# A fourth new order of the same 1382 steps in a one-core delta-rule and gated feed-forward kernel

## The chip, the cores and the metric

The kernel runs on one core of a Trainium2 chip. The metric is the time of one execution in microseconds (us) on the device; the time of a kernel is the median of its runs. The core has five engines that work at once, each taking its own instructions strictly in its own order: PE (TensorE, matrix products into the accumulation memory PSUM), DVE (VectorE), ACT (ScalarE), POOL (GpSimd), and SP (SyncE), which here only starts DMA transfers. An instruction waits until what it reads has been written and what it overwrites has been read, and everything behind it on the same engine waits with it.

## What is computed

A delta-rule attention layer (4 batches, 8 heads, 768 positions, 48 features a head) gives a matrix x of 3072 tokens by 384, and that goes through a gated feed-forward layer:

```python
k_n = k / (np.linalg.norm(k, axis=-1, keepdims=True) + 1e-06)
for t in range(S):
    y[:, :, t] = np.einsum('bhd,bhde->bhe', q[:, :, t], state)
    v_old = np.einsum('bhde,bhd->bhe', state, kt)
    state = state + bt[:, :, :, None] * np.einsum('bhd,bhe->bhde', kt, vt - v_old)
x = attn_out.transpose(0, 2, 1, 3).reshape(B * S, H * D)
a = x @ w1
b = x @ w2
h = a * b @ w3
return (h @ w_out).astype(np.float32)
```

Here kt, vt and bt are the normalised key, the value and the beta of position t. The weights w1 and w2 are 384 by 1024, w3 is 1024 by 1024, w_out 1024 by 384.

## The kernel before

The 768 positions are cut into 12 chunks of 64. Two chunks, of all batches and heads, make a pair; there are six pairs, called 0 to 5, and each gives 512 tokens of x for the feed-forward part. The work is written as generators, each cut by `yield` into steps; a step issues anything from one instruction to some tens on one engine. A string called ORDER lists 1382 steps by name, and the kernel is built by taking the next step of each name in the list. After the list has run, `in_text_order` ties every engine's instructions to the order in which they were written. So the list, and nothing else, sets what each engine does in which order; no scheduler moves anything afterwards. In this text g1.9 is the ninth step of the generator g1.

The generators that the prediction speaks of, with their lines:

- k, q, v, p: loads of keys, queries and values by SP. q1 is the load of the queries of chunk 1 into the tile X (L1233); the kernel needs it for Q1, their transposes on PE (L409).
- P0 to P35: pieces of the weights. Each is one load on SP (L838), two passes on ACT (L846, L849), one on DVE (L851) and one on POOL (L853). t transposes pieces of w3 on PE (L904), with a copy of the result on ACT (L907), and f folds w3 and w_out into one matrix on PE (L913).
- g squares the keys on POOL (L301) and sums the squares on DVE (L303); g.9 brings the sums of a pair together on PE (L286). N makes the norms from them, 15 short operations on DVE in a chain (L310 to L334), and the scale `wt` that the scores need.
- s makes the scores of a chunk: products on PE (L451, L457) into one of two large PSUM tiles ps_w, and from these on DVE U (L463) and PT (L474). u stores U to device memory (Ud, L491), V loads it again in another layout (Ub, L510) and then inverts the blocks in 31 pairs of DVE operations (L524, L529), shortest operands first and last; its result goes back through device memory to e, the corner products on PE (L619).
- n, c and y are the chain of states along the chunks on PE (L672) and DVE (L706, L717, L738), and its outputs (PE L777). y ends with four copies on ACT (L795) and six transfers that bring the feature rows of xT to their places (SP, L806).
- a and b are the products x@w1 and x@w2 (PE L934). Eight steps pairs of a, a20 to a27 for pair 2, make a round: a20.1 is the w1 product, a20.2 its copy by ACT (L946), a20.3 the w2 product, a20.4 the multiplication of the two on DVE (L950). Every product takes the next of four one-bank PSUM tiles ps_f, so a product waits until what the fourth product before it left there has been taken away.
- S are sums of slabs of a*b on POOL (L1007), o the products with the folded matrix on PE (L1166, seven to a pair), x the sums that make the results (DVE L1197, ACT L1201) and their stores on SP (L1182).
- The last pair does the products in another way (PE L1074, ACT L1088 to L1110, DVE L1083 to L1131).

The stages follow each other with overlap: loads and weights up to about 65 us, the products of pair 0 (a0, b) up to 146, the seven o of pair 0 and the states between up to 183, then for each pair a round of 16 products and a stretch of o, s, c and y, and from 496 us on the last pair.

Of the kernel before, what the change touches and what calls it, by code (L numbers as in the profile page):

```python
# [1358 lines left out]
```

## Time and profile before

| | us |
|---|---|
| three runs | 556.41, 562.43, 560.41 |
| their median | 560.41 |
| the profiled execution, first to last instruction | 556.1 |
| DVE busy in it | 343.7 (62%) |
| ACT busy in it | 145.7 (26%) |
| POOL busy in it | 169.7 (31%) |

The profiled execution is a separate one; its span stands 0.3 us under the fastest of the three runs and 4.3 us, 0.8%, under their median. The two lines that follow are of the page's part 2, the span in 40 slices of 13.9 us, each digit the busy share of a slice in tenths:

```profile
PE   6699999999999999999999999999999999989997
DVE  6799738589546498574995354885373973213552
```

PE is below nine tenths in the first two slices, once near the end and in the last slice. DVE is full in some slices, but in most it has room.

### The profile page before, as it was taken

Reading aid. Unit: us, or ns where it says so; the run is one execution under the profiler, and the core shown is the slowest. Engines: PE = TensorE matmul, PEld = TensorE weight load, DVE = VectorE, ACT = ScalarE, POOL = GpSimd, SP = SyncE. Lnnn points to the kernel's source line nnn. Section 1 sums busy time; section 2 is a strip of 40 time slices with the busy share of each in tenths; the row PEclk is TensorE's granted clock in tenths of the full one; section 3 lists DMA queues with packets and bytes.
Section 4 is the critical chain, followed back from the end, with each engine's and each line's share of the span. In section 5 each row is a group of like instructions: output and inputs, shape, how many; then the busy total and the mean of one; then the engine's idle time right before and its main releaser. Section 6 shows DMA issues by size and latency. Waiting matters only on the chain.

```text
span 556.1 us, 19932 instructions
## 1 busy us (share of the span) xinstructions
PE 533.6 (96%) x8732; PEld 390.8 (70%) x8732; DVE 343.7 (62%) x800; ACT 145.7 (26%) x291; POOL 169.7 (31%) x213
## 2 busy tenths in 40 slices
PE   6699999999999999999999999999999999989997
PEld 5556667788998544888444897445995447988897
DVE  6799738589546498574995354885373973213552
ACT  2786567531121120220111211202201102212200
POOL 7574443527730002812102522004540027420000
PEclk9999999999999999999999999999999999999999
DMA  9999956594423593453745453605307222020001
GB/s 189 339 307 230 158 140 150 128 160 55 96 48 55 119 147 72 67 88 89 122 74 100 70 91 80 126 38 83 51 15 154 26 60 38 18 58 1 0 2 57
DMA packets 191527, 54.22 MB, mean 98 GB/s; under 512 B 178928, under 2 KB 185072, under 8 KB 191440
## 3 DMA queue, kind: packets, MB, share of 16 engines
q1 hardware_dynamic: 189328, 52.56, 46.3%
q8 instruction: 68, 1.11, 0.9%
q10 hardware_dynamic: 2112, 0.39, 0.5%
q14 instruction: 19, 0.16, 0.1%
HBM read 41.78 MB, written 9.96 MB: 93 GB/s over the span
## 4 chain that ended last, share of the span: by engine, by line
PE 93%; DVE 3%; issue 2%; DMA 2%; ACT 0%; SPq 0%; DVEq 0%
PE ps_f L934 38%; PE ps_f L1166 20%; PE ps_f L913 7%; PE ps_w L672 6%; PE ps_w L777 4%; PE ps_f L1074 4%; PE ps_w L619 3%; PE ps_w L1074 2%; PE ps_w L451 2%; PE ps_f L369 1%; PE ps_w L457 1%; PE ps_f L904 1%; DMA beta_fm<-in_beta_dram 1%; PE ps_w L409 1%; PE ps_w L1166 1%
## 5 line engine op out<-in xcount | busy, mean ns | idle before, releaser
L934 PE MATMUL ps_f<-xT,w2s 128*128 128x512 f32 (+1 forms) x288 | 106.9, 524 | 0.0
L934 PE MATMUL ps_f<-xT,w1s 128*128 128x512 f32 (+1 forms) x288 | 106.7, 524 | 0.0
L934 PEld LDWEIGHTS ps_f<-xT,w2s 128*128 128x128 f32 x288 | 54.1, 190 | 46.5 <-issue 41.6
L934 PEld LDWEIGHTS ps_f<-xT,w1s 128*128 128x128 f32 x288 | 54.0, 190 | 45.3 <-issue 41.6
L1007 POOL TENSOR_TENSOR ab<-ab 128x256 f32<-128x256 f32 x80 | 56.4, 731 | 78.7 <-DVE ab L950 73.8
L946 ACT COPY ab<-ps_f 128x512 f32<-128x512 f32 (+1 forms) x48 | 24.3, 515 | 134.4 <-PE ps_f L934 130.3
L1166 PE MATMUL ps_f<-w,ab 128*128 128x192 f32 x320 | 57.3, 332 | 1.9 <-DVE osb L1197 1.3
L1166 PEld LDWEIGHTS ps_f<-w,ab 128*128 128x128 f32 x320 | 51.6, 190 | 3.3 <-issue 2.4
L524 DVE TENSOR_TENSOR tb<-Vb,Ub 128x31 f32<-128x31 f32 (+15 forms) x124 | 43.0, 347 | 15.4 <-DMA Ub<-Ud 11.5
L529 DVE TENSOR_TENSOR Vb<-Vb,tb 128x31 f32<-128x31 f32 (+15 forms) x124 | 43.0, 346 | 4.3
L913 PE MATMUL ps_f<-wo,w3T 128*128 128x384 f32 x128 | 43.5, 491 | 0.4 <-ACT w3T L907 0.4
L1166 PE MATMUL ps_f<-room,ab 128*128 128x192 f32 x240 | 42.8, 332 | 0.0
L950 DVE TENSOR_TENSOR ab<-ab,ps_f 128x512 f32<-128x512 f32 (+1 forms) x48 | 27.4, 589 | 24.0 <-PE ps_f L934 24.0
L1166 PEld LDWEIGHTS ps_f<-room,ab 128*128 128x128 f32 x240 | 38.7, 190 | 0.7
L913 PEld LDWEIGHTS ps_f<-wo,w3T 128*128 128x128 f32 x128 | 23.5, 190 | 15.4 <-ACT w3T L907 0.5
L301 POOL TENSOR_TENSOR sq<-ktok 128x384 f32<-128x384 f32 x24 | 19.7, 835 | 43.5 <-DMA out_dram<-osb 16.9
L658 POOL TENSOR_TENSOR vtok<-vtok,n 128x384 f32<-128x384 f32 x24 | 19.8, 832 | 39.5 <-DMA vtok<-in_v_dram 39.5
L635 ACT COPY T<-ps_w 32x512 f32<-32x512 f32 x24 | 13.8, 577 | 67.2 <-PE ps_w L619 46.2
L795 ACT COPY xT<-ps_w 112x256 f32<-112x256 f32 x48 | 14.3, 384 | 65.0 <-PE ps_w L777 61.7
L451 PE MATMUL ps_w<-KQ 48*64 48x128 f32 x320 | 21.9, 274 | 1.8 <-DVE PT L474 1.5
L717 DVE TENSOR_TENSOR X<-ps_w,wt 128x768 f32<-128x768 f32 x12 | 11.5, 956 | 19.4 <-PE ps_w L672 12.9
L1197 DVE TENSOR_TENSOR room<-room,ps_f 128x384 f32<-128x384 f32 (+1 forms) x13 | 7.0, 537 | 26.4 <-PE ps_f L1166 26.4
(170 smaller groups left out, 805.9 us busy)
## 6 DMA issues: line engine op xcount, KB each, us to landing
vtok<-in_v_dram SPq DMA_DIRECT2D x24, 192.0 KB, 4.4
out_dram<-osb SPq DMA_DIRECT2D x23, 192.0 KB, 2.6
ktok<-in_k_dram SPq DMA_DIRECT2D x44, 96.0 KB, 3.4
raw<-in_moe_w_dram SPq DMA_DIRECT2D x8, 512.0 KB, 6.2
raw<-in_moe_w_dram SPq DMA_DIRECT2D x18, 192.0 KB, 4.5
raw<-in_moe_w_out_dram SPq DMA_DIRECT2D x7, 384.0 KB, 5.3
Ud<-U SPq DMA_DIRECT2D x40, 64.0 KB, 2.8
Ub<-Ud SPq DMA_DIRECT2D x5, 512.0 KB, 4.2
```

Of the source, the lines that this page charges most:

```text
L451: pe.matmul(ps[half(z), 0, n : n + 128], lhsT=x[:, 0, :], rhs=x.rearrange("p j t -> p (j t)"), start=True, stop=True,)
L524: dve.tensor_tensor(out=tv, in0=V[:, 0 : s + 1, s : s + 1].to_broadcast([P, s + 1, n]), in1=U[:, s, s + 1 : BS].unsqueeze(1).to_broadcast( ...
L529: dve.tensor_tensor(out=o, in0=o, in1=tv, op=ALU.subtract)
L672: pe.matmul(out(ps, r, h, z), lhsT=lhs(r, h, z), rhs=rhs(r, h, z), start=True, stop=True,)
L777: i = pe.matmul(region(h, z, r), lhsT=lhs, rhs=rhs, start=part[n] not in part[:n], stop=part[n] not in part[n + 1 :],)
L913: pe.matmul(ps[:, 0:DM], lhsT=w3Ts[jc, kc // 4][:, kc % 4 * P : kc % 4 * P + P], rhs=wo(kc), start=(kc == 0), stop=(kc == KF - 1),)
L934: pe.matmul(ps[:].rearrange("p b c t -> p b (c t)"), lhsT=w[:, m, js], rhs=x[:, m, :, c0:c1].rearrange("p b c t -> p b (c t)"), start=(m = ...
L946: act.copy(out=t, in_=ps)
L950: dve.tensor_tensor(out=t, in0=t, in1=ps, op=ALU.mult)
L1007: (dve if u == last else pool).tensor_tensor(out=o_, in0=x_, in1=y_, op=op)
L1074: pe.matmul(ps[:, j, :], lhsT=w[j], rhs=x, start=first and j == 0, stop=j == 1, skip_group_check=not first,)
L1166: pe.matmul(ps[b][:, b, :], lhsT=ab_of(u, HF * f + i, t0), rhs=ws_[w][:, i], start=first and i == 0 and (b == 0 or n == "F"), stop=i == HF ...
```

## The change

The string ORDER is another arrangement of the same names. Every name stands in it as often as before; no generator, tile, buffer or instruction differs. The table of names is one line longer, so all code behind it carries a line number higher by one after the change (L934 becomes L935). The first lines of the table:

```diff
-k0 g0 g0 g0 K0 V0 g0 k1 P12 K0 K0 beta K1 P0 g0 g0 K1 K1 g0 q1 P12 g0 P12 P12 beta g0 g0 beta N0
+k0 K0 k1 K1 K0 K0 K0 g0 g0 g0 g0 g0 V0 s0 P13 P13 P13 P0 beta K1 P13 g0 g0 g0 g0 K1 P0 P0 P0 g0
...
```

Three places show what that does on the engines. The first is the start on SP. The rows are DMA issues in their order: `X<-in_q_dram` is the load q1, `raw`, `qperm`, `kperm` and `spare` are the buffers into which the pieces of w1, w2 and w3 (`in_moe_w_dram`) and of w_out come. Before:

```order
L233 DMA ktok<-in_k_dram 64x8x48 x4
L838 DMA raw<-in_moe_w_dram 128x1024
L1251 DMA beta_fm<-in_beta_dram 16x12x64 x2
L838 DMA raw<-in_moe_w_out_dram 128x768
L1233 DMA X<-in_q_dram 32x8x96 x4
L838 DMA raw<-in_moe_w_dram 128x1024
L838 DMA qperm<-in_moe_w_dram 128x1024
```

The same place after:

```order
L234 DMA ktok<-in_k_dram 64x8x48 x4
L839 DMA raw<-in_moe_w_dram 128x1024
L839 DMA raw<-in_moe_w_out_dram 128x768
L1252 DMA beta_fm<-in_beta_dram 16x12x64 x2
L839 DMA raw<-in_moe_w_dram 128x1024
L839 DMA raw<-in_moe_w_out_dram 128x768
L839 DMA qperm<-in_moe_w_dram 128x1024
L839 DMA raw<-in_moe_w_dram 128x1024
L839 DMA spare<-in_moe_w_out_dram 128x768
L839 DMA raw<-in_moe_w_out_dram 128x768
L1234 DMA X<-in_q_dram 32x8x96 x4
```

The queries of chunk 1 are loaded behind eight weight pieces, where they stood behind two.

The second place is PE near 87 us, around g1.9 (`ps_f<-ss,ident`, the sums from which N1 makes the scale of pair 1). Before, with the fold f6 (L913), the transposes Q3 (L369) and a state product c1.3 (L672) between it and the second scores step of s2 (L451, L457):

```order
L286 MATMUL ps_f<-ss,ident 64x16 x2
L913 MATMUL ps_f<-wo,w3T 128x384 x8
L369 MATMUL ps_f<-ident,X 48x2x32 x32
L672 MATMUL ps_w<-R,TT_89 64x48 x32
L451 MATMUL ps_w<-KQ 64x128 x2
L457 MATMUL ps_w<-KQ 64x64 x4
```

The same place after, with one product of b4 (L935) between it and the first scores step of s2:

```order
L778 MATMUL ps_w<-KQ,S 48x64 x16
L287 MATMUL ps_f<-ss,ident 64x16 x2
L935 MATMUL ps_f<-xT,w1s 128x256 x3
L452 MATMUL ps_w<-KQ 64x128 x2
L458 MATMUL ps_w<-KQ 64x64 x4
```

The fold, the transposes and the state product stand ahead of the sums now, and the outputs of y1 (L778) too.

The third place is PE before the products of round 2, from 250 us on: o1.5, o1.6 and o1.7 (L1166, with `room` or `w_117` the weights), the state products c5.3, c5.5 and c6.1 (L672) and the outputs y5.1 (L777), whose transfers fill the xT that round 2 (L934) reads. Before:

```order
L672 MATMUL ps_w<-R,TT_89 64x48 x32
L1166 MATMUL ps_f<-room,ab 128x192 x8
L777 MATMUL ps_w<-KQ,S 48x64 x16
L777 MATMUL ps_w<-PT,X 48x64 x32
L777 MATMUL ps_w<-KQ,S 48x64 x16
L1166 MATMUL ps_f<-room,ab 128x192 x8
L672 MATMUL ps_w<-X,ktok 48x48 x32
L1166 MATMUL ps_f<-w_117,ab 128x192 x8
L672 MATMUL ps_w<-S,KQ 64x48 x32
L286 MATMUL ps_f<-wt,ident 64x16 x2
L934 MATMUL ps_f<-xT,w1s 128x512 x9
```

The same place after:

```order
L1167 MATMUL ps_f<-room,ab 128x192 x8
L673 MATMUL ps_w<-R,TT_89 64x48 x32
L1167 MATMUL ps_f<-room,ab 128x192 x8
L778 MATMUL ps_w<-KQ,S 48x64 x16
L778 MATMUL ps_w<-PT,X 48x64 x32
L778 MATMUL ps_w<-KQ,S 48x64 x16
L673 MATMUL ps_w<-X,ktok 48x48 x32
L1167 MATMUL ps_f<-w_117,ab 128x192 x8
L673 MATMUL ps_w<-S,KQ 64x48 x32
L935 MATMUL ps_f<-xT,w1s 128x512 x3
```

Both o with `room` stand ahead of y5.1 now, where one stood behind it, the first of them ahead of c5.3 as well, and the small product with `ident` (N3.2) has moved out.

The rest, in words. In round 2 the first multiplication on DVE, a20.4, stands behind 18 of the 31 pairs of the inversion V3, where the first one, a25.4, stood behind 16; its product a20.3 is the second of the round, where a25.3 was the fourth. In round 3 the first multiplication stands behind all 31 pairs of V4 in both orders. On PE the products of a round come in another sequence in every round; the sequence within the last pair hardly differs.

More of the change, by code (lines that the diff above doesn't have):

```diff
@@ L64 @@
-x1 S1 x1 S1 y4 S1 y4 c5 o1 d7 d7 d7 d7 s7 s7 k8 g4 s7 s7 s6 s7 s7 u7 s6 s6 s6 s6 s6 c5 S1 c5 o1
-u6 y5 S1 x1 V3 o1 S1 x1 x1 c5 S1 y5 y5 S1 x1 V3 k9 S1 g4 c5 x1 x1 p8 V3 V3 V3 V3 V3 o1 c6 x1 V3
-V3 N3 N3 V3 V3 V3 V3 V3 V3 a27 a27 a25 x1 g4 a20 a25 a20 V3 V3 a25 a25 p8 a22 a22 V3 a24 a21 g4
-V3 V3 V3 a24 V3 d8 d8 p9 v6 V3 V3 a21 g4 g4 V3 V3 V3 V3 V3 V3 V3 V3 a22 a22 a27 a27 a20 n6 a20
-V3 e6 g4 a26 a26 a26 a24 d8 a21 n6 c6 e6 a26 d8 e7 a24 e6 e6 p9 g4 g4 g4 s8 N4 s8 a23 a23 s8 e6
-S2 e7 a21 e6 a23 a23 c6 e7 e7 c6 v7 o2 v9 o2 n7 n7 S2 y6 S2 S2 S2 V4 x2 K2 N4 c6 c6 o2 y6 e7 S2
@@ new lines @@
+d5 c3 n3 v5 c3 o0 x0 x0 x0 c3 c3 y3 y3 x0 x0 s4 N2 o0 s4 s4 s4 s4 s4 s5 s5 x0 s5 s5 s5 s5 y3
+a14 a16 a16 a14 a14 a14 c3 c3 a11 a15 a11 a15 u4 u5 V2 V2 v4 n4 n4 n5 n5 V2 a13 V2 V2 V2 V2 V2
+V2 p6 p6 x0 V2 V2 V2 V2 V2 V2 V2 V2 V2 V2 V2 V2 V2 V2 V2 V2 V2 V2 V2 V2 V2 V2 V2 a17 a17 a12
+a10 c4 a12 a13 d6 a10 a10 a10 S1 a12 a12 a17 a11 a11 a15 N2 a17 k6 g3 c4 g3 g3 g3 k7 g3 g3 g3
+a13 V2 e4 e4 e4 a15 a16 d6 d6 d6 g3 N2 g3 e4 e4 e4 a13 o1 c4 e5 e5 e5 e5 a16 V3 p7 S1 S1 S1 S1
+S1 o1 S1 c4 c4 g3 N3 x1 e5 e5 o1 c4 c5 c5 y4 y4 o1 p7 d7 d7 d7 d7 s7 s7 s7 s7 s7 s7 s6 s6 s6 s6
@@ new lines @@
+u7 s6 u6 x1 S1 S1 S1 S1 S1 S1 S1 x1 o1 x1 c5 c5 s6 o1 x1 y5 y5 c5 x1 S1 S1 o1 c5 c6 V3 V3 V3 x1
+x1 y5 V3 V3 V3 x1 x1 x1 k8 k9 V3 V3 V3 V3 V3 V3 V3 V3 g4 V3 V3 V3 V3 V3 a20 a20 a20 a20 a27 a22
+a22 a24 a24 a27 a24 a26 V3 V3 p8 d8 V3 a24 V3 V3 V3 V3 V3 V3 v6 n6 n6 c6 a26 a26 a26 d8 V3 V3
+p8 d8 d8 V3 a23 a23 a23 a23 a21 v8 V3 g4 g4 g4 a21 a21 a22 a27 g4 g4 S2 g4 g4 g4 V3 e6 e6 e6
+a22 a21 e6 a25 a25 a27 e6 e6 p9 p9 e7 v7 s8 N3 N3 g4 N4 s8 s8 o2 x2 c6 c6 a25 n8 a25 S2 S2 y6
+y6 e7 e7 S2 S2 S2 S2 o2 n8 S2 n7 c6 c6 S2 S2 V4 S2 n7 S2 o2 S2 S2 S2 S2 e7 e7 e7 c7 c7 o2 k11
@@ new lines @@
+c7 c7 d9 d9 s8 s8 u8 s8 x2 x2 o2 d9 d9 y7 y7 y7 x2 o2 x2 x2 s9 s9 s9 s9 o2 s9 u9 x2 x2 x2 x2 V4
+x2 a34 a34 a36 a31 a31 V4 V4 a36 a35 a35 V4 V4 V4 V4 V4 a30 a37 a37 V4 V4 a30 V4 V4 V4 V4 V4
+a32 a32 a33 a33 V4 V4 V4 V4 V4 V4 V4 V4 V4 V4 N4 N4 V4 V4 c7 V4 V4 V4 V4 V4 s9 a30 a30 a34 a34
+p10 d10 a35 a33 d10 a31 p10 a35 a36 k10 g5 g5 c7 c8 V4 e8 e8 e8 c8 g5 g5 a31 a33 a37 e8 e8 a37
+a36 a32 d10 d10 e9 e9 e9 a32 e8 c8 c8 e9 o3 x3 e9 e9 S3 S3 g5 g5 c8 c8 o3 S3 c9 o3 v9 g5 n9 g5
+n9 x3 c9 S3 S3 S3 S3 S3 g5 g5 y8 y8 S3 S3 p11 d11 d11 W p11 d11 c9 c9 v11 x3 N5 v10 n10 S3 S3
@@ L88 @@
+x4 x4 x4 S4 o4 a50 a51 X5 X5 x4 x4 X5 a50 a50 a50 a50 a50 a50 a50 a50 a50 a50 X5 a50 a50 a50
+a50 a50 a50 a50 a50 a50 a50 a51 a51 a51 a51 a51 a51 a51 a51 a51 a51 a51 a51 a51 a51 W a51 a51
+a51 a51 a51 a51 a52 a52 a52 a52 a52 a52 a52 a52 a52 a52 a52 a52 a52 a52 a52 a52 a52 a53 a53 a52
+a52 a52 a53 a52 a53 a53 a53 a53 a53 a53 a53 a53 a53 a53 a53 a53 a53 a53 a53 a53 o5 x5 a53 a53
+o5 S5 S5 o5 o5 S5 S5 K1 S5 S5 S5 S5 o5 x5 x5 x5 o5 x5 x5 x5 x5 x5 o5 x5 x5 Q3 K0 K2 x5 x5 K1 Q2
+Q1 Q2 x5
 """
```

65 lines of the change are left out of this document (24 added, 41 removed).

## The prediction, made before the changed kernel had run

> **What bounds the kernel now.** I read the page's engine line first, then the windows of busy time by stage, then PE's waits, and the timelines only where PE stands still. The engine line, with each engine's busy time:
>
> ```profile
> PE 533.6 (96%) x8732; PEld 390.8 (70%) x8732; DVE 343.7 (62%) x800; ACT 145.7 (26%) x291; POOL 169.7 (31%) x213
> ```
>
> A new order removes no work from PE, so all that it can give or take lies in the 556.1 - 533.6 = 22.5 us in which PE is idle. The windows say in which stages (columns: stretch, its length, busy us of PE, PE's weight loads, DVE, ACT and POOL, granted clock, DMA share, GB/s):
>
> ```profile
> 0.00:14.00 14.00, 8.62 (x220) 7.16 (x221) 8.76 (x21) 3.59 (x5) 9.99 (x22) 1.00 0.97 190
> 14.00:28.00 14.00, 8.30 (x324) 7.24 (x323) 10.88 (x30) 10.98 (x22) 7.30 (x7) 1.00 0.91 340
> 28.00:38.00 10.00, 9.48 (x34) 5.79 (x35) 9.62 (x30) 9.33 (x19) 7.28 (x7) 1.00 0.88 288
> 65.00:113.00 48.00, 46.25 (x1268) 35.28 (x1267) 25.29 (x55) 29.79 (x59) 18.70 (x17) 1.00 0.62 138
> 113.00:163.00 50.00, 49.51 (x727) 44.23 (x725) 34.59 (x91) 11.00 (x24) 28.79 (x36) 1.00 0.60 97
> 163.00:215.00 52.00, 50.86 (x712) 31.72 (x703) 36.04 (x95) 8.16 (x18) 0.00 (x0) 1.00 0.53 90
> 215.00:270.00 55.00, 53.27 (x1306) 41.58 (x1305) 37.17 (x88) 8.60 (x19) 19.30 (x27) 1.00 0.47 90
> 270.00:302.00 32.00, 32.00 (x128) 14.15 (x128) 25.49 (x58) 3.52 (x6) 4.91 (x6) 1.00 0.58 95
> 465.00:496.00 31.00, 29.37 (x789) 27.22 (x779) 7.17 (x12) 6.85 (x16) 12.15 (x18) 1.00 0.08 21
> 534.00:556.10 22.10, 18.55 (x114) 18.23 (x112) 9.08 (x16) 0.96 (x2) 0.00 (x0) 1.00 0.11 36
> ```
>
> 11.6 us are lost in the first 38 us, 1.75 from 65 to 113, 0.5, 1.1 and 1.7 in the next three stretches, nothing in round 2 itself, 1.6 before the last pair and 3.5 at the end. The largest losses by name:
>
> ```profile
> PE ps_w L409 <- issue: 5.4, 2, 4.4
> PE ps_f L1166 <- DVE osb L1197: 1.3, 1, 1.3
> PE ps_w L672 <- DVE X L717: 0.5, 1, 0.5
> ```
>
> So the path is PE from 28 us on, and the question is, stage by stage, whether PE still finds its operands and PSUM tiles ready. I count only PE's idle time, before and after.
>
> **A, the start (-1.0).** PE's rows there, then ACT's, then the sizes of the loads and their time to land:
>
> ```profile
> 21.37 1.06 PE L409 MATMUL ps_w<-KQ 48*32 48x64 f32 x52 [4.42 <-issue]
> 22.37 1.96 PE L369 MATMUL ps_f<-ident,X 64*48 64x64 f32 x64
> 28.05 2.85 PE L913 MATMUL ps_f<-wo,w3T 128*128 128x384 f32 x8 [0.43 <-ACT w3T L907]
> 31.36 1.09 PE L904 MATMUL ps_f<-ident,w 128*128 128x128 f32 x8 [0.47 <-POOL w L853]
> 40.56 1.11 PE L369 MATMUL ps_f<-ident,X 64*48 64x64 f32 x64
> ...
> 16.11 0.68 ACT L846 ACTIVATE w<-raw 128x512 f32<-128x512 f32 x1 [4.27 <-DMA raw<-in_moe_w_dram]
> 27.40 0.60 ACT L907 COPY w3T<-ps_f 128x512 f32<-128x512 f32 x1
> ...
> ktok<-in_k_dram SPq DMA_DIRECT2D x44, 96.0 KB, 3.4
> raw<-in_moe_w_dram SPq DMA_DIRECT2D x8, 512.0 KB, 6.2
> raw<-in_moe_w_out_dram SPq DMA_DIRECT2D x7, 384.0 KB, 5.3
> X<-in_q_dram SPq DMA_DIRECT2D x16, 96.0 KB, 4.9
> ```
>
> The fold f0 at 28.05 waits for ACT's copy at 27.40, and behind it PE loses 0.47 more. After the change ACT has about 1.7 us more ahead of that copy. But it waits less at 16.11: one pass pair of 1.1 us falls into the gap of 4.27, and the weight piece waited for has no q1 ahead of it (4 x 96 KB, 2.0 us at 190 GB/s). The copy comes at 26.0 to 28.0, and I take f0 at 28.0. PE has then done the 8.62 + 8.30 us of before and t5 (0.93) besides: idle 28.0 - 17.85 = 10.15, and 0.45 for the next transposed piece, where it was 11.6. The ends are -3.0 (copy at 26.0) and +1.5 (below).
>
> What q1's move costs: behind eight pieces it ends the first 4,736 KB (8 x 96 of keys, 4 x 512 and 4 x 384 of weights, 4 x 96 of its own), 4.85 MB. At 190 GB/s for 14 us, then 340, these are in at 14 + (4.85 - 2.66)/0.34 = 20.4 us. PE takes from Q1 to f0 22.37 to 28.05 less 0.43, and t5: 6.1 us. Q1 must start by 21.9. So q1 lies beside other work, by 1.5 us.
>
> The 4.42 us that end at 21.37 come from no operand that the trace shows. They may move with the order; the time they take lies ahead of the copy at 27.40 and gives nothing alone. The 64 transposes at 22.37 take 1.96 us, the same 64 at 40.56 take 1.11, while the windows give the clock as 1.00 in both. [...]
>
> **B, the second scores (+0.9).** From the sums g1.9 to the first U of s2, DVE's first and last row:
>
> ```profile
> 88.18 0.16 DVE L291 COPY ss<-ss 128x16 f32<-128x16 f32 x1
> 93.05 0.69 DVE L463 TENSOR_TENSOR U<-ps_w,wt 128x512 f32<-128x512 f32 x1
> ```
>
> This chain takes 4.9 us, and with U and PT (0.69 and as much) some 6.5 to 6.9 us from the sums until the first ps_w tile is free for s3. Before, a fold of 5.4 us covered it. Now PE has two half products b4.1 and b7.1 (1.3 each, half of a product below) and the two steps of s2 (0.95 each): 4.5. PE waits 2.0 to 2.4, I take 2.0. With 0.6 for corner products that come just behind their operands, this stage loses 2.6 instead of 1.75. Ends +0.3 and +1.5.
>
> **C, 113 to 183 us (-0.4).** The wait of L672 for DVE's X goes (0.5, the waits above), since o0.4 now stands between; y3.1 directly behind c3.3 brings most of it back, and N2 ahead of s4's multiplications makes s5.1 wait where s5.4 did. 1.3 instead of 1.7. Ends -0.8 and +0.3.
>
> **D, the way to round 2 (0).** PE's waits in this stretch, then what leads to xT (ACT's copies behind y5.1, SP's transfers, their landing), then the chain's row of a whole run of products:
>
> ```profile
> 250.37 1.15 PE L672 MATMUL ps_w<-R,TT 64*64 64x48 f32 x59 [0.20 <-DVE PT L474]
> 251.84 0.32 PE L672 MATMUL ps_w<-R,TT 64*64 64x48 f32 x5 [0.33 <-issue]
> 256.57 0.67 PE L777 MATMUL ps_w<-KQ,S 48*48 48x64 f32 x32
> 261.36 2.84 PE L1166 MATMUL ps_f<-w,ab 128*128 128x192 f32 x16 [0.46 <-DVE tb L524]
> ...
> 257.29 1.20 ACT L795 COPY xT<-ps_w 112x256 f32<-112x256 f32 x4 [13.52 <-PE ps_w L777]
> ...
> 258.51 4.22 SPq L806 DMA_DIRECT2D xT<-xT  x6
> ...
> xT<-xT SPq DMA_DIRECT2D x30, 32.0 KB, 2.0
> ...
> 265.36 36.25 PE ps_f L934 x84
> ```
>
> The three waits, 1.0 in all, go: with o1.5 and o1.6 ahead, operands and tiles are ready. But y5.1 ended at 257.24 and the fourth of its six transfers landed at about 258.51 + 3/6 x 4.22 + 2.0 = 262.6, 5.4 us later, the last 6.9 later. The first product needs the fourth, its end the sixth. Before, o1.6 (2.8) stood behind y5.1 too; now only c5.5, o1.7 and c6.1 do, 0.9 + 2.8 + 1.0 = 4.7. PE waits 0.7 to 2.2, I take 0.9: what was won is lost again. Ends -0.3 and +1.2.
>
> **E, round 2 (+0.2).** The rows of V3 on DVE (the first and the last of the pairs that matter, and one between), and POOL's at the same time:
>
> ```profile
> 263.74 0.25 DVE L524 TENSOR_TENSOR tb<-Vb,Ub 128x87 f32<-128x87 f32 x1
> 274.86 1.09 DVE L524 TENSOR_TENSOR tb<-Vb,Ub 128x256 f32<-128x256 f32 x1
> 278.62 0.42 DVE L529 TENSOR_TENSOR Vb<-Vb,tb 128x252 f32<-128x252 f32 x1
> ...
> 274.84 0.83 POOL L301 TENSOR_TENSOR sq<-ktok 128x384 f32<-128x384 f32 x1 [3.88 <-DVE Vb L529]
> ```
>
> a20.4 stands behind pair 18 of V3, and a24.3, the sixth product, wants the tile that a20.4 empties. V3's third pair comes at 263.2 (behind o1.7's last matmul and one sum). From 263.74 to 279.04 it took 15.3 us, 1.2 of which are other operations that have moved: 14.1, so the pair ends at 277.3 and a20.4 at 277.9. PE starts a20.1 at 265.36 less 0.5 (A to C), 0.2 (the small product that moved out) and the 1.0 of D, plus 0.9: 264.6. It comes to a24.3 five products of 2.59 later (36.25 / 14, six rows each), 277.5. The 1.09 at 274.86 is 0.66 over its neighbours and falls on the square on POOL. [...] I take 0.2, between nothing and 0.4; ends -0.2 and +1.5.
>
> **F and G, rounds 3, 4 and the last pair (+0.2, +0.2).** a31.3 waits for a tile that DVE empties just behind V4; in round 4 all tiles are free some us early; a50.3 has one product less to cover ACT's copy. The 1.3 us of L1166 on DVE's sums and the end's 3.5 keep their order. Each end -0.2 and +1.0.
>
> **The sum.** -1.0 + 0.9 - 0.4 + 0 + 0.2 + 0.2 + 0.2 = +0.1, so the profiled 556.1 become 556.2. The median of the runs stands 4.3 above that execution; 560.41 + 0.1 gives 560.5.
>
> **Rivals.** (1) Slower: q1 lands late. Past 21.9 us every us of q1 is a us of PE. For it: all of the eight pieces stand ahead of it on one queue, and a piece takes 5 to 6 us to land. Against: 340 GB/s were reached in this stretch. It decides from 21.9 on; landing at 28.0 costs 6.1: 566.6. (2) Slower, but less: V3 itself starts late, because its load of Ub stands behind a store of results on SP. Each us beyond a start of 263 is a us at a24.3 and again at the tiles behind it; 3 us give 563.5. Against: nothing in round 2 waits now. (3) Faster: the start runs without the 4.42 stall and the copies come early too: 11.6 idle becomes 6.5, 555.4. Against: ACT's row at 27.40 is full behind 16.11. (4) The change does nothing that can be seen is what I forecast; the moves on DVE, ACT and POOL are hidden behind a PE that is busy 96%.
>
> **Chances.** Forecast 0.62, within 557 and 564; rival 1 0.13; rival 2 0.12; rival 3 0.13. The three runs shown spread over 6 us, so a result can stand 2 to 3 us off by that alone. The range takes rival 3 to its time and rival 1 nearly to its: 555.0 to 566.5. A measurement tells about 1%, 5.6 us, from no change. Below 554.8 lies most of half of rival 3 and a spread: 0.10. Above 566.0 lie rival 1 and a part of rival 2: 0.16. Within: 0.74.
>
> **What would show it.** In the profile after: f0's first product at 28 (A right) or past 30 (rival 1, with PE's wait ahead of L369 named after the DMA into X); a wait of about 2 us of L451 on DVE's PT near 100; the waits at c5.3 and o1.7 gone and one of 0.7 to 2.2 us of the first L934 product on the xT transfers; at the sixth product of round 2 less than 1 us on DVE. PE's idle time altogether 22 to 23 us. I am wrong if it is below 18 or above 27.

## The result and the profile after

The kernel after takes 576.23 us (median of four runs, 575.20 to 577.52), the kernel before in the same session 559.73 (four runs, 556.41 to 562.43). The ratio is 1.0306, with a 95% interval of 1.0258 to 1.0354: slower by 3%, some 17 us. The forecast was 560.5, and 566.5 was the upper end of its range. In two of the experiments below (norms and q1 together; V1's late copy) some executions were slower than the rest (585.45 and 583.64 against 577.87 and 574.41 us; 583.19 against 573.88 to 577.60), so their ratios are of the others, and the trace of the first, taken in the one of 585.45, is used for its first 33 us and where it is named.

The profiled execution of after spans 573.5 us, 17.4 more than that of before. The engine line of its page, each engine with its busy time:

```profile
PE 537.2 (94%) x8732; PEld 391.3 (68%) x8732; DVE 355.3 (62%) x800; ACT 146.0 (25%) x291; POOL 171.2 (30%) x213
```

The same 8732 matmuls take 3.6 us more, and PE is idle for 573.5 - 537.2 = 36.3 us instead of 22.5. The windows of four stages (columns as in the prediction's: stretch, length, busy us of PE, its weight loads, DVE, ACT, POOL, granted clock, DMA share, GB/s) and the largest of PE's waits by name that grew or are new (us in all, times, longest):

```profile
0.00:14.00 14.00, 6.56 (x221) 5.58 (x222) 8.17 (x15) 5.52 (x9) 10.13 (x22) 1.00 0.92 217
14.00:28.00 14.00, 8.83 (x251) 7.62 (x250) 10.36 (x26) 7.09 (x14) 5.98 (x5) 0.51 1.06 339
28.00:38.00 10.00, 8.34 (x97) 5.70 (x98) 9.41 (x26) 9.94 (x21) 6.16 (x6) 1.00 0.88 254
...
113.00:163.00 50.00, 45.02 (x328) 39.11 (x326) 35.28 (x93) 6.99 (x18) 20.99 (x24) 0.97 0.54 86
...
PE ps_w L410 <- issue: 7.2, 2, 4.5
PE ps_f L935 <- DVE ab L951: 5.6, 2, 5.0
PE ps_w L620 <- issue: 1.8, 2, 1.0
PE ps_f L935 <- DMA xT<-xT: 1.7, 2, 0.9
PE ps_f L905 <- ACT KQ L380: 1.6, 1, 1.6
```

The first, in which PE waits for nothing that the trace shows, was there before and has grown from 5.4 to 7.2; the other four are new. The largest rise of idle time is in the last of these stretches, 5.0 us where before had 0.5.

Since the two kernels do their work in different order, windows of time compare unlike things. A better measure is the time that PE has lost up to a given step: the start of the step, less the time that the PE steps ahead of it took in the profiled execution of before. It holds idle time and slowed matmuls alike. The columns are the amounts of PE work that before has done at 40, 56, 70, 123, 145, 183 and 279 us, and the last product; all from the steps' starts in the traces.

| PE's lost time, us, up to | 40 | 56 | 70 | 123 | 145 | 183 | 279 | end |
|---|---|---|---|---|---|---|---|---|
| before | 12.0 | 11.6 | 11.7 | 13.3 | 13.3 | 15.0 | 16.7 | 19.0 |
| after | 15.1 | 15.4 | 16.4 | 20.4 | 27.2 | 29.4 | 33.6 | 36.7 |
| after, V1's second copy early | 15.3 | 15.0 | 16.0 | 20.3 | 20.4 | 22.8 | 27.1 | 31.2 |
| after, norms first | 17.8 | 18.9 | 19.8 | 23.4 | 31.7 | 33.4 | 37.6 | 41.0 |
| after, q1 early | 18.7 | 17.8 | 19.0 | 21.7 | 29.6 | 32.0 | 39.5 | 43.8 |
| before's order to f0.2 | 11.9 | 18.1 | 19.3 | 22.1 | 29.9 | 32.8 | 37.0 | 40.3 |
| the same, copy early, v1 and q2 late | 11.7 | 12.4 | 14.4 | 18.2 | 18.3 | 20.7 | 27.3 | 33.7 |
| before, v1 and q2 early | 11.6 | 13.9 | 13.9 | 15.2 | 15.2 | 16.6 | 17.7 | 20.1 |
| before's order to g1.9, copy early | 12.0 | 11.7 | 11.7 | 16.3 | 16.4 | 18.8 | 23.2 | 27.9 |
| before's order to c1.5, copy late | 12.0 | 11.7 | 11.5 | 19.4 | 27.2 | 29.9 | 34.0 | 37.8 |
| before's order to o0.1 | 11.9 | 11.6 | 12.1 | 14.2 | 14.2 | 17.8 | 21.4 | 25.0 |
| the same, y5.1 ahead of o1.6 | 11.7 | 11.4 | 11.3 | 12.6 | 12.6 | 15.7 | 23.1 | 28.8 |
| the same, all of y5 ahead of o1.6 | 11.6 | 11.3 | 11.0 | 13.2 | 13.2 | 20.5 | 31.9 | 35.3 |

After loses 17.7 us more than before: 3.1 by 40 us, 1.6 more by 70, 2.4 by 123, then 6.8 at once by 145 (27.2 - 20.4, where before lost nothing), and 3.8 behind that. Executions of one order differ too: the last three rows share their order up to o1.6, and stand 5 us apart at 183. In the last of them the granted clock was 0.57 from 176 to 184 us, 1.00 in the other two, and the 16 matmuls of an o there took 4.87 us, 3.03 in the first of the three. So a difference of a few us in this table says nothing without a row of a timeline behind it.

The start in the timeline of after (columns: start, length, instruction, and in brackets the idle time before it and what ended it), first PE, then DVE and POOL:

```profile
16.01 0.85 PE L410 MATMUL ps_w<-KQ 48*32 48x64 f32 x35 [4.50 <-issue]
16.79 0.40 PE L287 MATMUL ps_f<-ss,ident 64*64 64x16 f32 x4
17.12 1.45 PE L1259 MATMUL ps_f<-ident,beta_fm 16*128 16x16 f32 x12
18.50 1.37 PE L410 MATMUL ps_w<-KQ 48*32 48x64 f32 x77
22.61 1.06 PE L410 MATMUL ps_w<-KQ 48*32 48x64 f32 x51 [2.74 <-issue]
29.13 1.21 PE L905 MATMUL ps_f<-ident,w 128*128 128x128 f32 x8 [1.56 <-ACT KQ L380]
...
20.79 1.26 DVE L311 TENSOR_SCALAR seed<-ss 128x32 uint32<-128x32 uint32 x1
22.09 1.23 DVE L318 SCALAR_TENSOR_TENSOR nt<-ss,seed 128x32 f32<-128x32 f32 x1
...
20.74 1.28 POOL L854 TENSOR_TENSOR w<-w,raw 128x512 uint32<-128x512 uint32 x1 [0.42 <-ACT spare L850]
21.98 1.29 POOL L854 TENSOR_TENSOR w<-w,qperm 128x512 uint32<-128x512 uint32 x1
```

The first stall stands now inside s0.1, ahead of the sums of the keys (16.79, at 12.25 before) from which N0 makes the norms; a second one follows in s1. Two of N0's short operations take 1.2 us each, exactly beside POOL's work on weight pieces. N0 is done at 26.4, where it was at 16.6: 4.5 us of that lie ahead of its sums, 3.2 are passes over weight pieces that DVE does ahead of the chain, and 2.1 the two slow operations. The first fold starts at 32.06 instead of 28.05.

The second place is V1, the inversion of the next pair's blocks. SP's load, ACT's two copies of V1, DVE's first pair and the product that waits for it, from the timeline of after:

```profile
116.42 0.34 SPq L511 DMA_DIRECT2D Ub<-Ud  x1
...
120.98 0.60 ACT L519 COPY ps_w<-Vb 128x512 f32<-128x512 f32 x1
127.46 0.60 ACT L519 COPY ps_w<-Vb 128x512 f32<-128x512 f32 x1
...
128.09 0.19 DVE L525 TENSOR_TENSOR tb<-ps_w,Ub 128x31 f32<-128x31 f32 x1 [5.59 <-ACT ps_w L519]
...
147.65 3.24 PE L935 MATMUL ps_f<-xT,w2s 128*128 128x256 f32 x7 [4.97 <-DVE ab L951]
```

DVE has nothing else to do from 122.5 on, but the second of the two copies, step V1.4, stands on ACT behind the copies of four products (b1, b0, a04, b3), and each of these waits for PE. DVE stands still for 5.59 us. The multiplications of the products stand on DVE behind V1's pairs, so 20 us later PE waits 4.97 us for an emptied tile. The seven matmuls behind the wait are slow as well (last section): some 1.6 us more, which with the wait is nearly all of the 6.8.

The third place is the way to round 2:

```profile
275.16 1.20 ACT L796 COPY xT<-ps_w 112x256 f32<-112x256 f32 x4 [15.01 <-PE ps_w L778]
...
276.38 4.16 SPq L807 DMA_DIRECT2D xT<-xT  x6
...
280.81 1.10 PE L935 MATMUL ps_f<-xT,w1s 128*128 128x512 f32 x2 [0.77 <-DMA xT<-xT]
282.83 1.96 PE L935 MATMUL ps_f<-xT,w1s 128*128 128x512 f32 x4 [0.92 <-DMA xT<-xT]
```

The wait for xT that term D foresaw is there, 1.7 us.

### The profile page after: what moved, and what is told of

It is laid out like the page before. It is cut to its first block, busy times and chain, and to the rows that moved or that the text cites. A ratio compares the mean times of both kernels' runs of the same rounds, so it can differ in the third digit from the quotient of the medians.

```text
span 573.5 us, 19927 instructions
## 1 busy us (share of the span) xinstructions
PE 537.2 (94%) x8732; PEld 391.3 (68%) x8732; DVE 355.3 (62%) x800; ACT 146.0 (25%) x291; POOL 171.2 (30%) x213
## 3 DMA queue, kind: packets, MB, share of 16 engines
q8 instruction: 68, 1.11, 0.8%
## 4 chain that ended last, share of the span: by engine, by line
PE 72%; DVE 19%; issue 3%; DMA 3%; SPq 1%; ACT 1%; POOL 0%; DVEq 0%; POOLq 0%; ACTq 0%
PE ps_f L935 29%; PE ps_f L1167 18%; DVE tb L525 5%; PE ps_w L673 5%; PE ps_w L778 4%; PE ps_f L1075 4%; DVE ps_w L530 3%; PE ps_w L1075 2%; PE ps_w L620 2%; DVE Vb L530 2%; PE ps_f L914 2%; PE ps_w L452 1%; DMA raw<-in_moe_w_dram 1%; PE ps_w L458 1%; DVE w L852 1%
## 5 line engine op out<-in xcount | busy, mean ns | idle before, releaser
L935 PE MATMUL ps_f<-xT,w2s 128*128 128x512 f32 (+1 forms) x288 | 109.3, 531 | 5.6 <-DVE ab L951 5.6
L935 PE MATMUL ps_f<-xT,w1s 128*128 128x512 f32 (+1 forms) x288 | 106.7, 524 | 1.7 <-DMA xT<-xT 1.7
L935 PEld LDWEIGHTS ps_f<-xT,w2s 128*128 128x128 f32 x288 | 54.9, 194 | 51.6 <-issue 40.1
L935 PEld LDWEIGHTS ps_f<-xT,w1s 128*128 128x128 f32 x288 | 54.0, 190 | 47.8 <-issue 44.7
L302 POOL TENSOR_TENSOR sq<-ktok 128x384 f32<-128x384 f32 x24 | 20.1, 847 | 111.0 <-DVE tb L525 40.4
L525 DVE TENSOR_TENSOR tb<-Vb,Ub 128x31 f32<-128x31 f32 (+15 forms) x124 | 44.4, 358 | 11.2 <-DMA Ub<-Ud 7.4
L530 DVE TENSOR_TENSOR Vb<-Vb,tb 128x31 f32<-128x31 f32 (+15 forms) x124 | 45.0, 363 | 4.3
L951 DVE TENSOR_TENSOR ab<-ab,ps_f 128x512 f32<-128x512 f32 (+1 forms) x48 | 27.3, 590 | 19.4 <-PE ps_f L935 19.3
L914 PEld LDWEIGHTS ps_f<-wo,w3T 128*128 128x128 f32 x128 | 23.4, 190 | 15.6 <-ACT w3T L908 0.7
L525 DVE TENSOR_TENSOR tb<-ps_w,Ub 128x31 f32<-128x31 f32 (+15 forms) x62 | 21.1, 340 | 7.2 <-ACT ps_w L519 5.6
L739 DVE TENSOR_TENSOR S<-S,ps_w 112x768 f32<-112x768 f32 x10 | 9.5, 952 | 21.8 <-PE ps_w L673 21.6
L530 DVE TENSOR_TENSOR ps_w<-ps_w,tb 128x31 f32<-128x31 f32 (+15 forms) x62 | 21.7, 349 | 2.1
```

The lines of the kernel that those rows point to most:

```text
L302: pool.tensor_tensor(out=sq[:], in0=kt[:, r], in1=kt[:, r], op=ALU.mult)
L525: dve.tensor_tensor(out=tv, in0=V[:, 0 : s + 1, s : s + 1].to_broadcast([P, s + 1, n]), in1=U[:, s, s + 1 : BS].unsqueeze(1).to_broadcast( ...
L530: dve.tensor_tensor(out=o, in0=o, in1=tv, op=ALU.subtract)
L914: pe.matmul(ps[:, 0:DM], lhsT=w3Ts[jc, kc // 4][:, kc % 4 * P : kc % 4 * P + P], rhs=wo(kc), start=(kc == 0), stop=(kc == KF - 1),)
L935: pe.matmul(ps[:].rearrange("p b c t -> p b (c t)"), lhsT=w[:, m, js], rhs=x[:, m, :, c0:c1].rearrange("p b c t -> p b (c t)"), start=(m = ...
L951: dve.tensor_tensor(out=t, in0=t, in1=ps, op=ALU.mult)
```

## The experiments

Each kernel is an arrangement of the same steps, with one exception that is named; V1.4 is the fourth step called V1, and so on. Line numbers differ by one or two from those of after. The ratios are to the kernel before in the same session (557.8 to 558.5 us). A diff shows the names of ORDER around the moved ones, or tells of which parts a mixed order is made.

**V1's second copy.** V1.4 stands directly behind V1.3.

```diff
- V1 V1 P24 b1 b1 a04 b0 b0 a04 b3 b3 V1 a01 a01
+ V1 V1 V1 P24 b1 b1 a04 b0 b0 a04 b3 b3 a01 a01
```

> The changed kernel with one step moved: the second copy of V1's start matrix into PSUM (L519, ACT) directly behind the first, ahead of the products b1, a04, b0 and b3 and their copies on ACT. Theory 1: this copy, at 127.46, held V1 from 120.6 (the load of Ub landed) to 128.09, and with it the first multiplication behind V1, for which PE waited 4.97 us and then ran one product at half speed. Then V1's first pair comes at 121 to 123, the wait of L935 on DVE's ab near 147 goes, and the time falls by 6 to 7 us, to about 569.5 (ratio to before about 1.018). Rival: V1 is late because PE and the scores ahead of it are late by 7 us; then the wait shrinks by the copy's 0.6 us at most and the time stays within 574 to 577.

Measured: 569.72 us, ratio 1.0200 (1.0164 to 1.0235), span 567.9. ACT's copies, DVE's first pair and PE's product in its timeline:

```profile
120.84 1.22 ACT L517 COPY ps_w<-Vb 128x512 f32<-128x512 f32 x2
...
122.27 0.18 DVE L523 TENSOR_TENSOR tb<-ps_w,Ub 128x31 f32<-128x31 f32 x1
...
139.67 2.86 PE L933 MATMUL ps_f<-xT,w2s 128*128 128x256 f32 x12
```

Both copies are made at once, DVE waits for nothing, and PE's wait of 5 us is gone: the lost time does not rise between 123 and 145 us. One step on ACT makes about 6 us of the 17: 6.5 by the medians of two sessions, 5.5 by the lost time at the end (36.7 - 31.2).

**The norms first.** The sums, the transposed betas and N0 stand ahead of s0 and of the weight pieces.

```diff
- V0 s0 P13 P13 P13 P0 beta K1 P13 g0 g0 g0 g0 K1 P0 P0 P0 g0 P8
+ V0 beta g0 g0 g0 g0 g0 beta beta N0 s0 P13 P13 P13 P0 K1 P13 K1 P0 P0 P0 P8
```

> The changed kernel with the norm of pair 0 first: the sums g0, the transposed betas and N0 stand ahead of s0 on PE and ahead of the weight pieces on DVE, as they do in the kernel before; q1 stays behind eight pieces. Theory 1: the late start comes from N0, which ended at 26.4 instead of 16.6 because its sums stood behind PE's stall of 4.50 us and its 15 operations behind five weight passes on DVE; ACT's copy for V0 then waited for U, and the copies of the transposes behind it. Then N0 ends by 17, V0's first pair comes at 26 to 27 instead of 31.94, the first fold at 28 to 29 instead of 32.06, and the time falls by 3 to 4 us, to about 572.5. Rival 1: the queries' load behind eight pieces sets the start; then the first fold stays within 1 us of 32 and the time at 576. Rival 2: the stalls that come from no operand set it; then they grow by what N0 gains and the fold stays past 31.

Measured: 580.44 us, ratio 1.0404 (1.0359 to 1.0450): slower than after. N0 is done at 17.8 us as meant, but PE's transposes Q1 come later, and the first fold at 34.91, outside what the theory and the first rival had:

```profile
26.97 0.42 PE L368 MATMUL ps_f<-ident,X 64*48 64x64 f32 x2 [6.14 <-DMA X<-in_q_dram]
```

The DVE passes over the weight pieces now stand behind N0, and POOL's behind those, so POOL was done with the raw tile that P1 takes over only at 21.7. On SP, q1 stood behind P1's load, which was issued at 21.69. What was won for the norms, q1 lost.

**q1 early.** q1 stands ahead of P8's load.

```diff
- K1 P0 P0 P0 g0 P8 P8 P8 P8 P3
+ K1 P0 P0 P0 g0 q1 P8 P8 P8 P8 P3
```

> The changed kernel with the load q1 moved back ahead of the second weight piece, nothing else. Theory 1 (N0 sets the start): the first fold stays at 32 to 33 and the time within 575 to 578. Rival 1 (q1 sets it): Q1's transposes come before 22 instead of at 23.60, the first fold at 29 to 30, and the time falls by 2 to 3 us.

Measured: 581.33 us, ratio 1.0411 (1.0367 to 1.0455). q1's four transfers have landed by 15.4 us; in after they land at 22.0 to 23.6. Yet Q1 starts at 22.75 instead of 23.60, behind the same stall, so the late q1 held it by 0.85 us at most. The weights are later, t1 waits 2.95 us for ACT where it waited 1.56, and the first fold starts at 33.57, so the rival falls; but the time is over the theory's range too. Part of that is slow matmuls: the granted clock is 0.50 from 28 to 38 us, 1.00 in after, and the 16 matmuls of the fold take 7.69 us instead of 5.43.

**The start of before.** The order of before up to f0.2 (some 38 us), that of after behind it.

> The order of before up to the second half of the first fold (f0.2, about 35 us), and all other steps behind it in the order of after. If each stage adds its own loss, PE's idle time up to 40 us is the 11.6 us of before instead of 14.8, and the time falls by 3 to 4 us, to about 572.5; the losses from 60 to 90 us (4.3 us more than before) and behind V1 (6.8) stay. If the later losses are only the start's delay carried on (weights that come late, V1 late), they fall too, and the time comes to 560 to 565.

Measured: 578.91 us, ratio 1.0345 (1.0283 to 1.0407). The start is as good as before's (11.9 us lost at 40), and yet 6.2 us are lost by 56 us and nothing is won in the end, so neither of the two forecasts holds. PE's longest wait there, and ACT's queue at the same time:

```profile
58.81 1.43 PE L368 MATMUL ps_f<-ident,X 64*48 64x64 f32 x44 [3.40 <-ACT w L919]
...
53.97 0.67 ACT L845 ACTIVATE w<-spare 128x512 f32<-128x512 f32 x1 [3.73 <-DMA spare<-in_moe_w_dram]
```

ACT waits for a weight piece that lands late, and the copy of a fold, which PE needs, stands behind that pass.

**The order of before to g1.9, that of after behind it, copy early.** In this mixture the steps of y0 and y1 and of the weight pieces 25, 26, 29 and 34 take each other's tiles, so the part that goes through them is not the reference's; the instructions are the same.

> The order of before up to step g1.9 (some 99 us), that of after behind it, and the second copy of V1 directly behind the first, as in the run with that copy moved. Theory (the loss has two parts, the first 100 us and V1's late copy; what comes behind them is worth 4 to 6 us): idle time of PE as before up to 100 us, V1's 5 us wait gone, 563 us (561 to 565.5). Rival (the start's loss is only put off, since what stands behind it waits for the same loads): 567 or more.

Measured: 566.78 us, ratio 1.0140 (1.0095 to 1.0184), 1.3 us over the range of the theory and at the edge of the rival's. The lost time says which: 11.7 at 70 us as in before, 3 us at the seam of the two orders (1.91 for no releaser ahead of y1, 1.29 at s3), nothing at V1. Apart from the seam, the first part's loss is not put off; it is gone.

**The loads of v1 and q2.** The start of before and the early copy, and v1 and q2 put behind the weights' loads.

```diff
- P16 P16 P16 v1 P22 P23 q2 P23 P15 P15 P15 P15 n1 ... P26 P26 f1 ... v0 n0
+ P16 P16 P16 P22 P23 P23 P15 P15 P15 P15 ... P26 q2 P26 f1 ... v0 v1 n1 n0
```

> The run with the start of before up to f0.2, with V1's second copy directly behind the first, and with the loads of v1 and of q2 put behind the weights' loads (v1 behind v0, q2 behind P26). Theory (behind a restored start, v1 and q2 ahead of P22 to P26 on SP's queue make the weights land late; ScalarE waits for them in its order and holds back the copies of f and KQ): of the 572.4 us that the late start's run would have with the copy moved, 5 to 8 go: 564.4 to 567.4, and the waits of h0 and t3 (4.3 and 1.9 us) shrink below 1 each. Rival (the order of the pairs of V0 and of the weights' passes on VectorE sets it): 571 to 574.

Measured: 571.05 us, ratio 1.0214 (1.0165 to 1.0263), the time of the rival. But in its trace ACT takes the same piece, 6 us earlier, without waiting:

```profile
47.99 0.68 ACT L845 ACTIVATE w<-spare 128x512 f32<-128x512 f32 x1
```

PE lost 0.7 us between 40 and 56 us instead of 6.2. So the loads were the cause there, and the time was lost again later: between 183 us and the end this kernel loses 13.0 us, the run with the start alone 7.5. 4.1 of the 13.0 lie at a20, where the first product waits 2.35 us for xT, 1.73 in the run with the start alone. Most of the difference between the two runs is slow matmuls: the six behind that wait take 4.31 us instead of 2.81, and 16 of o4 near 493 us 4.55 instead of 2.87, with a granted clock of 0.71 and 0.66 in these stretches. The rest is open.

**The same two loads moved in before**, alone.

```diff
- P14 P22 P17 P23 P21 ... P20 q2 P27 k2 v0 q3 v1
+ P14 v1 P22 P17 P23 q2 P21 ... P20 P27 k2 v0 q3
```

> The kernel before with two loads alone moved, as in after: v1 behind P14 and q2 behind P23. Theory (loads of 384 KB ahead of the weights make these late): ScalarE waits for P22, P23, P15 or P17, and PE idles 2 to 5 us more between 38 and 65 us: ratio 1.004 to 1.01. Rival (there is room in the queue; loads alone do nothing): ratio 0.998 to 1.002.

Measured: 558.79 us, ratio 1.0024 (0.9995 to 1.0053). The waits appear as the theory had them, ACT for a piece and PE for ACT behind it:

```profile
49.70 0.66 ACT L845 ACTIVATE w<-raw 128x512 f32<-128x512 f32 x1 [3.95 <-DMA raw<-in_moe_w_dram]
...
58.12 1.24 PE L912 MATMUL ps_f<-wo,w3T 128*128 128x384 f32 x3 [1.29 <-ACT w L919]
```

PE has lost 2.3 us more at 56 us (13.9 against 11.6), but at the end only 1.1, and in the time none of it can be told from nothing. Before's order has room behind these loads.

**Five weight pieces late.** P0, P8, P3, P9 and P12 stand behind s1.3, to quieten the DMA engines during s0.

> The kernel after with the five weight pieces P0, P8, P3, P9 and P12 (2.2 MB of loads and their passes) behind step s1.3, so that the DMA engines are idle for much of the time between 10 and 17 us. Theory (PE's instructions come over the same DMA engines, in portions of 128 matmuls, and stand behind the bulk loads): the stall of 4.50 us in s0.1, behind its 93rd matmul, shrinks to under 1.5 us, and N0 ends by 20 us instead of 26.4. Rival (the stall belongs to that place in the program, whatever the DMA engines do): it stays between 3.5 and 5 us. The whole gets slower in both, since the weights come late: 580 us or more.

Measured: 587.05 us in one run, and a stall of 3.96 us at the same matmul. This settles nothing on the theory: SP waits for no step of another engine there and issued the loads between 10.55 and 14.69 all the same. It shows N0 without weights beside it, though. POOL has no weight work from 14 to 24 us, the operation that took 1.26 us takes 0.17, and N0 ends at 22.1.

**Norms first and q1 early**, both together; the diff is to the run with the norms first.

```diff
- P12 P12 P12 P12 P9 P2 P2 P2 P1 P1 q1 s0 s0
+ P12 P12 P12 P12 P9 q1 P2 P2 P2 P1 P1 s0 s0
```

> The order of after, with the norms (g0.6 to g0.10, beta, N0) ahead of s0 and of the weight pieces, as in an earlier run, and in addition the load of q1 ahead of P2's. Theory (the start's 4 us are two things, either of which alone leaves the other: N0 stands behind the stalled s0.1, and q1 stands behind a load that waits for its buffer): Q1 starts by 23 us, f0's first product at 28 to 29.5, where after has 32.1. The whole time is then 573 to 579, since what is won there was lost again behind 40 us in the run with the start of before. Rival (the passes over the weight pieces hold f0 back, whatever N0 and q1 do): f0 at 31 us or later.

Measured: ratio 1.0328 (1.0281 to 1.0375), some 576 us by the 557.76 of before. Q1 starts at 22.97 as expected, but the first fold at 32.23: the transposed pieces ahead of it wait for POOL (0.99) and for ACT (0.34), and the eight transposes of each take 1.97 us. The time is in its range, the step is not; the rival's bound of 31 holds. Moving N0 and q1 together does not give the start back. ACT's rows show what is left. Its copies for V0, Q1 and the transposed pieces stand behind one another. In after the first of them waits 2.05 us for U and comes at 27.97. Here it does not wait for U, but it stands behind passes over weight pieces that landed late (one wait of 1.97) and comes at 27.07; in before it comes at 21.48, ahead of these pieces.

**The order of before up to o0.1 (some 146 us)**, that of after behind it.

> The order of before up to step o0.1 (some 146 us, V1 among it), that of after behind it. Theory (the order of after behind V1 costs 4 to 6 us by itself, some 2 of them at a20's transfers of xT): 562 us (560.5 to 564.5), ratio 1.005 to 1.011; PE idle within 1 us of before up to 150 us, and 23 to 25 us in all. Rival (the losses behind V1 are only echoes of a late first part): ratio within 0.997 to 1.003.

Measured: 565.31 us, ratio 1.0130 (1.0099 to 1.0161), over the range. PE's lost time: 14.2 at 145 us, 25.0 at the end, so 10.8 in the part of after, where before loses 5.7. The order behind V1 costs 5 us by itself, 7.5 by the medians.

**y5.1 put back ahead of o1.6** in that kernel.

```diff
- o1 x1 c5 c5 s6 o1 x1 y5 y5 c5
+ o1 x1 c5 c5 s6 y5 o1 x1 y5 c5
```

> The same with y5.1 put back ahead of o1.6 as well, the place that it had in before. Theory (PE's wait for xT ahead of a20 comes from y5.1's later place): the wait of some 2.5 us at a20 shrinks to under 0.7, the whole is 1.5 to 2.5 us shorter than the run without this. Rival (xT's transfers are held by other work on SP's queue or by ScalarE's copies): the wait stays over 1.5.

Measured: 568.23 us, ratio 1.0194 (1.0164 to 1.0224), slower than without. PE's wait for xT hardly shrinks, from 1.78 to 1.47 us, and SP's rows show why:

```profile
264.30 0.38 SPq L1181 DMA_DIRECT2D out_dram<-osb  x1
264.74 4.80 SPq L805 DMA_DIRECT2D xT<-xT  x6
```

ACT's copy was done at 261.6. But the transfers are y5's later steps, and on SP they stood behind a store of results, which waits for DVE's sums. At y5.1 PE now waits 1.68 us for DVE's PT. Most of what this trace loses besides is slow matmuls, not the order: the six behind the wait for xT take 4.51 us, 2.81 without the move, and this row

```profile
488.40 4.55 PE L1165 MATMUL ps_f<-w,ab 128*128 128x192 f32 x16
```

took 2.87 us without it, in the same place behind the same wait of 1.24.

**The first nine weight loads cut to a sixteenth.** Only here does an instruction differ; the columns left out are set to zero.

```diff
+ FEW = (13, 0, 8, 3, 9, 12, 2, 1, 10)
+ k = n // 16 if i in FEW else n
+ if k < n:
+     dve.memset(raw[:, k:n], 0)
- out=raw[rows, 0:n].rearrange("p n w -> p (n w)"), in_=src.bitcast(U32)
+ out=raw[rows, 0:k].rearrange("p n w -> p (n w)"), in_=src[:, 0:k].bitcast(U32)
```

> The kernel after with the loads of the first nine weight pieces (13, 0, 8, 3, 9, 12, 2, 1, 10) cut to a sixteenth of their columns, the rest of the raw tile set to zero on VectorE: this part of the weights is left out of what is computed. The DMA engines have little to do between 9 and 20 us. Theory (PE's instructions come in portions of 128 matmuls over the same DMA engines, and the bulk loads make them late): the stall of 4.50 us in s0.1 shrinks to under 1.5, that of 2.74 in s1.1 to under 1. Rival (the portions come at their own pace, whatever else is transferred): the stalls stay within 0.7 us of 4.5 and 2.7, at the same counts of matmuls.

Measured: 585.88 us in one run, since the zeroing stands in VectorE's queue and ACT waits for it. The two stalls in its timeline of PE:

```profile
12.06 0.54 PE L410 MATMUL ps_w<-KQ 48*32 48x64 f32 x35 [0.25 <-issue]
18.14 1.06 PE L410 MATMUL ps_w<-KQ 48*32 48x64 f32 x51 [1.39 <-issue]
```

They stand behind the same matmuls, the 93rd of s0.1 and the 77th of s1, and shrink from 4.50 to 0.25 us and from 2.74 to 1.39, while the DMA engines moved 93 GB/s from 8 to 20 us instead of 330. The second stays over the 1 us expected. So the bulk loads make the stalls long, and the count of matmuls decides where they stand.

**All of y5 ahead of o1.6.** Product, copy and transfers.

```diff
- o1 x1 c5 c5 s6 o1 x1 y5 y5 c5 x1 ... x1 x1 y5 V3 V3
+ o1 x1 c5 c5 s6 y5 y5 y5 o1 x1 c5 x1 ... x1 x1 V3 V3
```

> The order of before up to o0.1, that of after behind it, and all three steps of y5 (product, copy, transfers) ahead of o1.6 and of the store x1.5, where the run with y5.1 alone moved left the transfers behind that store. Theory (the transfers of xT are late by y5's place, and y5.1 alone could not help because SP held its transfers behind the store): xT is issued within 1.5 us of ScalarE's copy, PE's wait at a20 is under 0.7 us, and the time is 1 to 2 us under the run that leaves y5 as in after. Rival (SP or the DMA engines are late there for another reason): the wait at a20 stays over 1.5 us.

Measured: 572.90 us, ratio 1.0251 (1.0215 to 1.0287), worse still. Rows of SP, DVE and PE:

```profile
266.41 3.74 SPq L805 DMA_DIRECT2D xT<-xT  x6
270.20 0.58 SPq L509 DMA_DIRECT2D Ub<-Ud  x1
...
275.81 0.19 DVE L523 TENSOR_TENSOR tb<-Vb,Ub 128x31 f32<-128x31 f32 x1 [5.82 <-DMA Ub<-Ud]
...
273.12 2.84 PE L933 MATMUL ps_f<-xT,w1s 128*128 128x512 f32 x6
291.58 4.45 PE L933 MATMUL ps_f<-xT,w2s 128*128 128x512 f32 x6 [3.75 <-DVE ab L949]
```

xT comes straight behind ACT's copy and the first product waits for nothing: the theory of what makes xT late holds, though its time does not. V3's load of Ub now stands behind xT on SP, DVE waits 5.82 us for it ahead of V3, and PE waits for DVE at a24.3. That is the mechanism of the prediction's second rival (there Ub stood behind a store), at the product that term E had named. Of the 10.3 us that this trace loses more than the one without the move, 2.7 lie ahead of 183 us, where the order is the same.

**V1's late copy behind the first part of before** (the order of before up to c1.5, some 104 us).

> The order of before up to step c1.5 (some 104 us), that of after behind it, with V1's second copy at its late place. Theory (V1's wait is made by the copy's place on ScalarE alone, whatever the first 100 us took): PE waits 4 to 7 us for VectorE at a00.3, PE idle is as in before up to 110 us and 5 to 7.5 us more from there to 140 us; the time is 568 to 573. Rival (it is an echo of the late first part, and with the first part of before VectorE reaches V1's pairs in time): no wait over 1.5 us there, 563 to 566.

Measured: ratio 1.0316 (1.0282 to 1.0349), some 576 us by the 558.46 of before, more than expected. DVE's first pair and the waiting product:

```profile
127.06 0.19 DVE L523 TENSOR_TENSOR tb<-ps_w,Ub 128x31 f32<-128x31 f32 x1 [5.59 <-ACT ps_w L517]
...
146.62 3.35 PE L933 MATMUL ps_f<-xT,w2s 128*128 128x256 f32 x7 [4.97 <-DVE ab L949]
```

The wait is the same to a hundredth of a us as in after, though the first 104 us were those of before. 7.8 us are lost there (19.4 to 27.2), and 7.9 between 70 and 123 us (before 1.6), most of it at the seam, where ACT waits 5.43 us for a weight piece and PE 3.29 for ACT. V1's loss does not come from a late first part.

No kernel tried here beats before.

## Why the prediction was wrong

The time was forecast as before's, and 17.7 us of PE's lost time were added.

**What bounds the kernel.** That PE's idle time is the quantity to sum was right. The tests that the prediction set itself spoke at once: f0 at 32.06 (past 30) and an idle time of 36.3 (over 27). But the list of places at which the sum looked for lost time was too short.

**C (113 to 183 us): -0.4 forecast, +7.3 measured.** This is the step that failed most. The term looked at two small waits between states and scores. V1, which runs on DVE through this stretch, and ACT's two copies that it needs stand nowhere in the sum; the trace of before shows both copies 4 us ahead of need (107.42 and 109.11, the first pair at 113.21), so the move behind four product copies could have been priced by their waits for PE. The early copy and the run with the late copy behind before's first part show it from both sides.

**A (the start): -1.0 forecast, +3.1 measured.** ACT's copy that f0 needs was to come at 26.0 to 28.0; it came at 31.40. The 4.42 us were expected to move and to cost nothing by themselves. They moved: in after a stall stands ahead of N0's sums, and with the weight passes on DVE it brings N0 9.8 us and the U of the first scores 7.1 us later; U is what ACT's copies wait for. The loads were mis-sized too: q1 was to be in at 20.4 and was in at 23.59, past the bound of 21.9, since its transfers took 7.9 to 9.4 us each. PE shows no wait for it, because the second stall holds PE until 23.6 as well, and with q1 early it gains 0.85 us; so rival 1 is not the cause. Restoring before's order up to f0.2 restores the time lost there; restoring the norms, q1 or both does not. In the last case ACT's copies stand behind weight pieces that land late. That these passes make the 3 us was not tested by a run of its own.

**Between A and B (40 to 70 us): no term, +1.6 measured.** The weights' loads, with v1 and q2 ahead of some, bind here as soon as the start is quick, and that is why the start alone gave nothing. In after the late start covers part of it; which wait makes the 1.6 there was not tested.

**B (second scores): +0.9 forecast, +2.4 measured for 70 to 123 us.** The wait of 2 us on PT behind N1 did not come as such. In its place PE waits at the corner products (L620), 1.8 us in two stalls for nothing that the trace shows, which before did not have there. The last section counts the matmuls between them; why they are long there, where before passes the same counts without one, is open.

**D (the way to round 2): 0 forecast, +2.5 measured from 183 to 279 us.** The wait for xT is 1.7 us, inside the 0.7 to 2.2 given, and the waits at c5.3 and o1.7 went. The taken value of 0.9 was too small, and 0.63 is lost ahead of it, at a15.3, a product of round 1 that waits for DVE and that the term did not see; the rest has no single wait. That the place of y5's steps makes xT late is shown; putting them back gave no time back in either of two runs, and part of what these lost is slow matmuls (six took 4.51 us instead of 2.81 in the one, six took 4.45 instead of 2.84 in the other).

**E, F, G: +0.6 forecast, +0.8 measured.** The number fits, but partly by luck. a24.3 does not wait in after, and of the waits named for the later rounds none appears; instead c11.1, ahead of the last pair, waits 1.24 us for the state that DVE updates (L739), which no term had. No run shows the lower end of E's "between nothing and 0.4", for which V3 had to come earlier: in after a square on POOL at 287.76 still stood beside a V3 operation ahead of a20.4, which took 0.93 us where its neighbours take 0.42; before had two such (0.90 and 1.09).

**The rivals.** The first (q1 late) is worth 0.85 us at most. The third (no stall at the start) fell, the stalls grew. The second did not happen in after, but did when y5 was moved whole. A rival with its cause in ACT's queue was missing.

## What to carry to other kernels

When a change moves a whole order, list for each engine the steps that stand behind something which waits for another engine, the small copies on ScalarE above all: one copy behind four that wait for TensorE cost about 6 us of 17. Price a moved transfer on its whole queue, with all steps that belong to it, and with what it will stand ahead of: both attempts to bring xT earlier made the kernel slower. And a loss that is undone in one place (the start here) shows in the end only if no other queue binds just behind it; measure the lost time at several points of the work, not only the end. Before a loss of 1 to 3 us is put down to an order, compare the durations of the same matmuls in both traces: the seven matmuls behind V1's wait, at a granted clock of 0.50, took 1.6 us longer here, and the 16 of o4 1.7 us longer in four traces out of fourteen.
